# The first 60 microseconds of an attention and feed-forward kernel: first loads, first weight and small constants in another order

## The chip, the cores and the metric

The kernel runs on one core of a Trainium2 chip. The metric is the device time of one execution in microseconds; the median of three runs of the kernel before is 783.38 us (783.3 to 783.8). The engines of the core, TensorE (matrix products), VectorE, ScalarE, GpSimd and SyncE, each work through their own list of instructions, and meet by semaphores. Transfers between main memory and the on-chip memory are issued by GpSimd, SyncE or ScalarE and carried out by 16 DMA engines.

## The reference

```python
# q, k, v: (4, 6080, 256)
qn = q / (norm(q, axis=1) + 1e-6);  kn = k / (norm(k, axis=1) + 1e-6)
s = kn.transpose(0, 2, 1) @ qn / tau          # (4, 256, 256), tau = 1
a = softmax(s, axis=-1)
x = (v @ a).reshape(24320, 256)
h = x @ w_in                                  # (256, 2048)
g = s_scale * relu(h) ** 2 + b
out = g @ w_out                               # (2048, 256)
```

The attention runs over the 256 channels: per batch, a sum over 6080 tokens gives one 256 x 256 matrix and the norms of each channel of q and k. All inputs are float32, and so is the output.

## The kernel before

**The work and its tiles.** Per batch the matrix `a` is multiplied into `w_in` first ("fold", lines 231 to 246), so that the main loop takes v straight to the hidden layer with the folded weight `wa`. The constant b becomes a row that is added at the end (`rowconst`, b times the column sums of w_out), and the scale s is applied, with that row, when the output leaves the accumulator (line 449).

The main loop goes over groups of 512 tokens, and in each over 16 blocks of 128 hidden features: a step. A step is two matmuls of 512 columns (`mm1`, line 417), ScalarE's Relu (line 420), VectorE's square (line 427), and, four and five steps later, four matmuls of 256 columns into the output (`mm2`, line 441). Everything else for later is hung into this loop as side work for a given step: v loads and transposes, the Gram matrices, norms and folds of the next batch, the casts of w_out to float16 (lines 321 to 326), and the sums for `rowconst` (lines 330 to 339).

**The front.** Batch 0 has to be done before the loop can begin. Its q and k come in eight chunks (five of 1024 tokens, then 512, 256 and 192). Per chunk TensorE adds to the Gram matrix `s_ps` (line 120), ScalarE squares k (143), VectorE squares q (140) and adds the squares up by halves (156). After the last chunk comes a chain: 40 tiny matmuls sum the squares over tokens (`n_ps`, 185), a square root, a reciprocal, the scaled matrix `sm_s` (201), its transposes `t_ps` (208), the exponentials `eT` (214), their sums `r_ps` (223), and sixteen fold matmuls, in eight pairs of 512 columns, each evacuated to `wa` by ScalarE or VectorE in turn (242, 244). The transposes of the first v tile (272) stand between `t_ps` and the sums.

**What sets the order.** Nearly every instruction is pinned by `po` to the written order on its engine; the constants outside it are placed by a scheduler. All large loads go out from GpSimd on one software queue, in this order: eight times k and q (which the DMA converts to float16), w_in, v0, w_out in two halves, v1, v2, then v3 and the k and q of batch 1. A GpSimd load waits until the eighth before it has landed. `s_bc` and `b_bc`, the broadcast scalars s and b, come on SyncE's queue at the very start.

**Buffers.** `h_ps` has four accumulator buffers, which h, the folds, the transposes and the norm sums share; the relu result r has three; k and q tiles have six. w_out lands as float32 in `w_out32` (16 x 256 per partition).

Of the kernel before, what the change touches and what calls it, by code (L numbers as in the profile page):

```python
# [10 lines left out]
FP32 = mybir.dt.float32  # L11
AF = mybir.ActivationFunctionType
# [4 lines left out]
def kernel(  # L17
# [12 lines left out]
    nc = tc.nc  # L30
    P = 128

    B, N, C = q.shape
    Dff = moe_w_in.shape[1]
# [7 lines left out]
    LAM = 16.0  # L42
    EPS = 1e-6

    CH = C // P
    FT = Dff // P
    TG = 512
# [4 lines left out]
    def po(ins):  # L52

        tc.keep_in_program_order(ins)
        return ins
# [39 lines left out]
    class Gram:  # L95


        def __init__(self, b, chunks):
            self.b, self.chunks = b, chunks
            self.tiles = {}  # L100
            self.rows = []

        def load(self, c):
            at, np_, jc = self.chunks[c]
            kc = qk_pool.tile([P, JC, C], FP16, tag="kc", name="kc")
            qc = qk_pool.tile([P, JC, C], FP16, tag="qc", name="qc")
            for t, src in ((kc, k), (qc, q)):
                po(nc.gpsimd.dma_start(  # L108
                    out=t[:np_, :jc, :],
                    in_=src[self.b, at : at + np_ * jc, :].rearrange("(p j) c -> p j c", j=jc)))  # L110
# [18 lines left out]
        def norm_ops(self, c):  # L129
# [43 lines left out]
                ops += [fold(4, slice(0, 1), False), fold(4, slice(1, 2), False)]  # L173
            return ops + [fold(2, slice(0, 2), False), fold(1, slice(0, 2), True)]

        def finish_ops(self):

            st = {}

            def norms():  # L180
                n_ps = ps_h.tile([P, 2, CH], FP32, tag="h_ps", name="n_ps")
                todo = [(t, np_, j, a, ch) for t, np_, jc in self.rows for j in range(jc)
                        for a in range(2) for ch in range(CH)]
                for i, (t, np_, j, a, ch) in enumerate(todo):
                    po(nc.tensor.matmul(n_ps[:, a, ch : ch + 1], t[:np_, a, j, ts(ch, P)],  # L185
                                        ones16[:np_, 0:1], start=(i == 0),
                                        stop=(i == len(todo) - 1), skip_group_check=True))
                nrm = sm_pool.tile([P, 2, CH], FP32, tag="nrm", name="nrm")
                po(nc.scalar.activation(out=nrm, in_=n_ps, func=AF.Sqrt))
# [13 lines left out]

            def turn():
                st["t"] = ps_h.tile([P, CH, C], FP32, tag="h_ps", name="t_ps")
                for j in range(CH):
                    for ch in range(CH):
                        po(nc.tensor.transpose(  # L208
                            st["t"][:, j, ts(ch, P)], st["s"][:, ch, ts(j, P)], ident32))

            def exps():
                st["e"] = sm_pool.tile([P, CH, C], FP16, tag="eT", name="eT")
                for j in range(CH):
                    po(nc.scalar.activation(  # L214
                        out=st["e"][:, j, :], in_=st["t"][:, j, :], func=AF.Exp,
                        scale=st["r"][:, 0, j : j + 1]))
                self.wa = apool.tile([P, CH, Dff], FP16, tag="wa16", name="wa16")

            def sums():
                r_ps = ps_h.tile([P, CH], FP32, tag="h_ps", name="r_ps")  # L220
                for ch in range(CH):
                    for j in range(CH):
                        po(nc.tensor.matmul(r_ps[:, ch : ch + 1], st["e"][:, j, ts(ch, P)],
                                            ones16[:, 0:1], start=(ch == 0 and j == 0),
                                            stop=(ch == CH - 1 and j == CH - 1),
                                            skip_group_check=True))
# [4 lines left out]
            NW = 512  # L231

            def fold_w(fo, m):
                def f():
                    wa_ps = ps_h.tile([P, NW], FP32, tag="h_ps", name="wa_ps")
                    for j in range(CH):
                        po(nc.tensor.matmul(wa_ps, st["e"][:, j, ts(m, P)],  # L237
                                            w_in16[:, j, ds(fo * NW, NW)],
                                            start=(j == 0), stop=(j == CH - 1)))
# [18 lines left out]
    def load_v(g):  # L258
        t0, nj = group(g)
        v16 = vpool.tile([P, TG // P, C], FP16, tag="v16", name="v16")  # L260
        po(nc.gpsimd.dma_start(  # L261
            out=v16[:, :nj, :],
            in_=v_flat[t0 : t0 + nj * P, :].rearrange("(p j) c -> p j c", j=nj)))
        v_tiles[g] = v16
# [10 lines left out]
        vT_tiles[g] = vT  # L275


    grams = {b: Gram(b, chunks_first if b == 0 else chunks_later) for b in range(B)}
    g0 = grams[0]
    for c in range(len(g0.chunks)):  # L280
        g0.load(c)
    po(nc.gpsimd.dma_start(out=w_in16, in_=moe_w_in.rearrange("(co p) f -> p co f", p=P)))
    load_v(0)
    w_out_rows = moe_w_out.rearrange("(fo p) d -> p fo d", p=P)
    for h in range(2):
        po(nc.gpsimd.dma_start(out=w_out32[:, ts(h, FT // 2), :], in_=w_out_rows[:, ts(h, FT // 2), :]))
    load_v(1)
    load_v(2)
    ident16 = consts.tile([P, P], FP16)
    make_identity(nc, ident16)  # L290
    ident32 = consts.tile([P, P], FP32)
# [2 lines left out]
    nc.vector.memset(ones16, 1.0)  # L294
    ones32 = consts.tile([P, P], FP32)
    nc.vector.memset(ones32, 1.0)
    s_bc = consts.tile([P, 1], FP32)
    nc.sync.dma_start(out=s_bc, in_=moe_s.to_broadcast((P, 1)))
    b_bc = consts.tile([P, 1], FP32)
    nc.sync.dma_start(out=b_bc, in_=moe_b.to_broadcast((P, 1)))  # L300
    s_out = consts.tile([P, 1], FP32)
    nc.vector.tensor_scalar_mul(out=s_out, in0=s_bc, scalar1=1.0 / (LAM * LAM))


    warm = consts.tile([P, 1], FP32)
    po(nc.scalar.activation(out=warm, in_=ones32[:, 0:1], func=AF.Sqrt))
    g0.start()
    for c in range(len(g0.chunks)):
        ops = g0.norm_ops(c)
        for j in range(g0.chunks[c][2]):  # L310
            g0.mm(c, j)
        for f in ops:
            f()
    fin = g0.finish_ops()
    for f in fin[:3]:
        f()
    transpose_v(0)
    for f in fin[3:]:
        f()

    def cast_w_out(i):
        part = slice(i * FT // 8, (i + 1) * FT // 8)
        if i % 2:
            po(nc.scalar.copy(out=w_out16[:, part, :], in_=w_out32[:, part, :]))
        else:
            po(nc.vector.tensor_copy(out=w_out16[:, part, :], in_=w_out32[:, part, :]))

    cast_w_out(0)

    def rowconst_sum(i, n):  # L330
        w = w_out32.rearrange("p f c -> p (f c)")
# [173 lines left out]
```

## Time and profile before

| | |
|---|---|
| median of three runs | 783.38 us |
| profiled execution, its time / span | 782.96 / 781.2 us |
| TensorE matmuls busy | 753.2 us (96%) |
| VectorE, ScalarE busy | 505.2, 517.8 us |
| main memory read, written | 78.9 MB, 24.9 MB |
| landing of k0, q0; of q4; of v0 | 8.3, 10.9; 30.6; 42.0 us |
| first matmul of the main loop | 47.58 us |
| first matmul into the output | 49.74 us |
| the rowconst matmul | 62.24 us |

A line of a group gives the code line, engine and operation, output and inputs with their shapes, the count, then busy time and the mean of one in ns, then the idle time of the engine just before such instructions and what ended it. Lines of the chain and the timeline begin with the start and length in us. The lines of stretches give for each engine the busy time and the count, in the order TensorE matmul, weight load, VectorE, ScalarE, GpSimd, and then TensorE's granted clock, the DMA engines' busy share and GB/s.

### The profile page before, as it was taken

Reading aid. Unit: us, or ns where it says so; the run is one execution under the profiler, and the core shown is the slowest. Engines: PE = TensorE matmul, PEld = TensorE weight load, DVE = VectorE, ACT = ScalarE, POOL = GpSimd, SP = SyncE. Lnnn points to the kernel's source line nnn. Section 1 sums busy time; section 2 is a strip of 40 time slices with the busy share of each in tenths; the row PEclk is TensorE's granted clock in tenths of the full one; section 3 lists DMA queues with packets and bytes.
Section 4 is the critical chain, followed back from the end, with each engine's and each line's share of the span. In section 5 each row is a group of like instructions: output and inputs, shape, how many; then the busy total and the mean of one; then the engine's idle time right before and its main releaser. Section 6 shows DMA issues by size and latency. Waiting matters only on the chain.

```text
span 781.2 us, 14420 instructions
## 1 busy us (share of the span) xinstructions
PE 753.2 (96%) x5646; PEld 527.4 (68%) x5646; DVE 505.2 (65%) x1106; ACT 517.8 (66%) x858; POOL 57.2 (7%) x111
## 2 busy tenths in 40 slices
PE   2689999999999999999999999999999999999997
PEld 2456777767677777776667667776667766666666
DVE  3767676676656766666566666766566565565565
ACT  3466666666766666766766666666676666666665
POOL 3410010001000010000001000000000000000000
PEclk9689999999999999999999999999999999999999
DMA  8999425115535164124715645131113113121011
GB/s 158 212 263 186 96 44 130 41 41 101 131 76 115 41 133 95 41 42 85 145 41 96 129 85 108 46 75 45 41 48 74 42 42 83 42 52 51 28 55 42
DMA packets 22421, 66.34 MB, mean 85 GB/s; under 512 B 2752, under 2 KB 3328, under 8 KB 22352
## 3 DMA queue, kind: packets, MB, share of 16 engines
q0 software_dynamic: 15152, 40.51, 29.4%
q1 hardware_dynamic: 7200, 24.91, 9.8%
q8 instruction: 44, 0.72, 0.4%
q14 instruction: 25, 0.20, 0.1%
HBM read 78.91 MB, written 24.90 MB: 133 GB/s over the span
## 4 chain that ended last, share of the span: by engine, by line
PE 93%; DMA 5%; issue 1%; ACT 1%; DVE 0%; POOL 0%; POOLq 0%
PE o_ps L441 42%; PE h_ps L417 42%; PE s_ps L120 4%; DMA qc<-in_q_dram 4%; PE vT_ps L272 3%; PE wa_ps L237 2%; DMA v<-in_v_dram 1%; ACT r L420 0%; PE n_ps L185 0%; ACT eT L214 0%; PE t_ps L208 0%; ACT L214 0%; DVE o_sb L449 0%; PE rc_ps L338 0%; POOL kc L108 0%
## 5 line engine op out<-in xcount | busy, mean ns | idle before, releaser
L420 ACT ACTIVATE r<-h_ps 128x512 f16<-128x512 f32 (+1 forms) x768 | 450.0, 593 | 225.8 <-PE h_ps L417 199.9
L427 DVE TENSOR_TENSOR g<-r 128x512 f16<-128x512 f16 (+1 forms) x768 | 321.9, 420 | 243.4 <-ACT r L420 236.6
L441 PE MATMUL o_ps<-w_out,g 128*128 128x256 f16 x3040 | 456.8, 273 | 0.0
L417 PE MATMUL h_ps<-vT,wa 128*128 128x512 f16 (+7 forms) x1632 | 453.0, 364 | 0.6 <-ACT r L420 0.6
L441 PEld LDWEIGHTS <-g 128*128 128x128 f16 x3040 | 295.2, 98 | 183.0 <-DVE g L427 0.2
L417 PEld LDWEIGHTS <-wa 128*128 128x128 f16 x1632 | 157.9, 98 | 30.0 <-issue 0.8
L120 PE MATMUL s_ps<-qc,kc 128*128 128x256 f16 (+1 forms) x384 | 72.9, 296 | 18.5 <-DMA qc<-in_q_dram 18.5
L449 DVE SCALAR_TENSOR_TENSOR o_sb<-o_ps,s_out,rowconst 128x512 f32<-128x512 f32 x95 | 71.1, 748 | 6.4 <-PE o_ps L441 5.6
L261 POOL DMA_DIRECT2D v<-in_v_dram x48 | 25.7, 535 | 617.0 <-PE vT_ps L272 597.6
L143 ACT ACTIVATE sq<-kc 128x1024 f16<-128x1024 f16 (+3 forms) x49 | 50.0, 1031 | 21.9 <-DMA kc<-in_k_dram 18.7
L120 PEld LDWEIGHTS <-kc 128*128 128x128 f16 (+1 forms) x384 | 40.2, 106 | 26.8 <-issue 10.2
L140 DVE TENSOR_TENSOR sq<-qc 128x1024 f16<-128x1024 f16 (+3 forms) x49 | 32.6, 675 | 11.1 <-DMA qc<-in_q_dram 11.1
L274 DVE COPY vT<-vT_ps 128x1024 f16<-128x1024 f16 (+1 forms) x48 | 32.5, 677 | 4.3 <-PE vT_ps L272 4.3
L156 DVE TENSOR_TENSOR f<-sq 128x1024 f16<-128x1024 f16 (+1 forms) x47 | 31.8, 685 | 0.3
L272 PE MATMUL vT_ps<-ident,v 128*128 128x128 f16 x380 | 29.5, 221 | 2.0 <-DMA v<-in_v_dram 2.0
L272 PEld LDWEIGHTS <-v 128*128 128x128 f16 x380 | 25.5, 99 | 3.5 <-DMA v<-in_v_dram 2.4
L156 DVE TENSOR_TENSOR f<-f 128x512 f16<-128x512 f16 (+3 forms) x47 | 25.8, 550 | 0.4
L237 PE MATMUL wa_ps<-w_in,eT 128*128 128x512 f16 x64 | 18.9, 398 | 0.0
L242 ACT ACTIVATE wa<-wa_ps,rs 128x512 f16<-128x512 f32 x16 | 11.0, 687 | 7.6 <-PE wa_ps L237 4.3
L108 POOL DMA_DIRECT2D qc<-in_q_dram x26 | 14.2, 548 | 13.7 <-DMA qc<-in_q_dram 7.7
L108 POOL DMA_DIRECT2D kc<-in_k_dram x26 | 14.2, 548 | 11.4 <-DMA kc<-in_k_dram 9.1
L244 DVE TENSOR_SCALAR wa<-wa_ps,rs 128x512 f16<-128x512 f32 x16 | 11.9, 745 | 1.4 <-PE wa_ps L237 1.2
(37 smaller groups left out, 55.9 us busy)
## 6 DMA issues: line engine op xcount, KB each, us to landing
out_dram<-o_sb SPq DMA_DIRECT2D x47, 512.0 KB, 3.7
v<-in_v_dram POOLq DMA_DIRECT2D x47, 256.0 KB, 5.1
kc<-in_k_dram POOLq DMA_DIRECT2D x20, 512.0 KB, 8.1
qc<-in_q_dram POOLq DMA_DIRECT2D x20, 512.0 KB, 10.0
w_out<-in_moe_w_out_dram POOLq DMA_DIRECT2D x2, 1024.0 KB, 13.2
kc<-in_k_dram POOLq DMA_DIRECT2D x3, 480.0 KB, 8.4
qc<-in_q_dram POOLq DMA_DIRECT2D x3, 480.0 KB, 10.3
w_in<-in_moe_w_in_dram POOLq DMA_DIRECT2D x1, 1024.0 KB, 12.5
```

What stands on the lines that cost most here:

```text
L120: po(nc.tensor.matmul(self.s_ps[:, ch, :], kc[:np_, j, ts(ch, P)], qc[:np_, j, :], start=(c == 0 and j == 0 and ch == 0), stop=(c == len(s ...
L140: po(nc.vector.tensor_mul(st["sq"][:np_, 0, js, :], qc[:np_, js, :], qc[:np_, js, :]))
L143: po(nc.scalar.activation(out=st["sq"][:np_, 1, js, :], in_=kc[:np_, js, :], func=AF.Square))
L156: po(nc.vector.tensor_add(st["f", half][:np_, arrays], src[:np_, arrays, :half, :], src[:np_, arrays, half : 2 * half, :]))
L237: po(nc.tensor.matmul(wa_ps, st["e"][:, j, ts(m, P)], w_in16[:, j, ds(fo * NW, NW)], start=(j == 0), stop=(j == CH - 1)))
L272: po(nc.tensor.transpose(vT_ps[:, ch, ts(j, P)], v16[:, j, ts(ch, P)], ident16))
L274: po(nc.vector.tensor_copy(out=vT[:, :, : nj * P], in_=vT_ps[:, :, : nj * P]))
L417: po(nc.tensor.matmul(dst, wa[:, ci, ts(m, P)], src, start=(ci == 0), stop=(ci == CH - 1), skip_group_check=True))
L420: po(nc.scalar.activation(out=r16[:, :n], in_=h_ps[:, :n], func=AF.Relu))
L427: po(nc.vector.tensor_mul(g16[:, :n], r16[:, :n], r16[:, :n]))
L441: po(nc.tensor.matmul(o_halves[g, h][:, j % 2, :], g16[:, ts(j, P)], w_out16[:, m, :], start=(m == 0 and j == js[0]), stop=(m == FT - 1 an ...
L449: po(nc.vector.scalar_tensor_tensor(out=o_sb[:, js[0] : js[-1] + 1, :], in0=o_halves.pop((g, h)), scalar=s_out, op0=ALU.mult, in1=rowconst ...
```

## The change

- The first k and q go out from SyncE's and ScalarE's hardware queues, as float32, into the buffer of w_out, which is still empty; VectorE casts k and ScalarE casts q to float16.
- The identity matrices are made on GpSimd ahead of the loads instead of after them.
- w_in is loaded in two pieces: its first 512 columns, then v0, then the other 1536. Only the first block of the weight is folded ahead of the loop; the other six folds are side work of steps 1, 2, 5, 6, 9 and 10. The casts of w_out move from the place before the loop and steps 0 to 6 to steps 2 to 9.
- The norm sums of all chunks but the last stand before the last chunk's Gram matmuls: 32 of the 40 tiny matmuls go ahead of it, eight stay behind.
- Eight matmuls whose result nobody reads (`keep_busy`) stand in the chain: six ahead of the transposes `t_ps`, two ahead of the sums.
- `s_bc` and `b_bc` are loaded from GpSimd's queue, after v2; `s_out`, computed from `s_bc` on VectorE, is now pinned after the first two folds.

```diff
@@ class Gram
+            direct = self.b == 0 and c == 0
+            for i, (t, src) in enumerate(((kc, k), (qc, q))):
+                rows = src[self.b, at : at + np_ * jc, :].rearrange("(p j) c -> p j c", j=jc)
+                if direct:
+                    raw = w_out32[:, ds(i * JC, JC), :]
+                    (nc.sync, nc.scalar)[i].dma_start(out=raw, in_=rows)
+                else:
+                    po(nc.gpsimd.dma_start(out=t[:np_, :jc, :], in_=rows))
...
+        def cast(self, c):
+            qc, kc = self.tiles[c]
+            for h in range(2):
+                js = slice(h * JC // 2, (h + 1) * JC // 2)
+                po(nc.vector.tensor_copy(out=kc[:, js, :], in_=w_out32[:, js, :]))
+                po(nc.scalar.copy(out=qc[:, js, :],
+                                  in_=w_out32[:, JC + js.start : JC + js.stop, :]))
...
+        def add_norms(self, last=False):
+            first = self.n_ps is None
+            if first:
+                self.n_ps = ps_h.tile([P, 2, CH], FP32, tag="h_ps", name="n_ps")
+            todo = [(t, np_, j, a, ch) for t, np_, jc in self.rows for j in range(jc)
+                    for a in range(2) for ch in range(CH)]
+            self.rows = []
...
@@ the front
-    for c in range(len(g0.chunks)):
-        g0.load(c)
-    po(nc.gpsimd.dma_start(out=w_in16, in_=moe_w_in.rearrange("(co p) f -> p co f", p=P)))
-    load_v(0)
...
-    nc.sync.dma_start(out=s_bc, in_=moe_s.to_broadcast((P, 1)))
-    nc.sync.dma_start(out=b_bc, in_=moe_b.to_broadcast((P, 1)))
-    nc.vector.tensor_scalar_mul(out=s_out, in0=s_bc, scalar1=1.0 / (LAM * LAM))
...
+    g0.load(0)
+    po(nc.scalar.activation(out=warm, in_=ones32[:, 0:1], func=AF.Sqrt))
+    g0.cast(0)
+    for c in range(1, len(g0.chunks)):
+        g0.load(c)
+    load_w_in(0, NW)
+    load_v(0)
+    load_w_in(NW, Dff)
     for h in range(2):
         po(nc.gpsimd.dma_start(out=w_out32[:, ts(h, FT // 2), :], in_=w_out_rows[:, ts(h, FT // 2), :]))
+    load_v(1)
+    load_v(2)
+    po(nc.gpsimd.dma_start(out=s_bc, in_=moe_s.to_broadcast((P, 1))))
+    po(nc.gpsimd.dma_start(out=b_bc, in_=moe_b.to_broadcast((P, 1))))
...
+        if c == NCH0 - 1:
+            g0.add_norms()
...
+    def keep_busy(n):
+        idle_ps = ps_h.tile([P, TG], FP32, tag="h_ps", name="idle_ps")
+        for _ in range(n):
+            po(nc.tensor.matmul(idle_ps, w_in16[:, 0, :P], w_in16[:, 0, :NW],
+                                start=True, stop=True, skip_group_check=True))
...
-    for f in fin[:3]:
-        f()
-    transpose_v(0)
-    for f in fin[3:]:
-        f()
+    fin[0]()
+    fin[1]()
+    keep_busy(6)
+    fin[2]()
+    transpose_v(0)
+    keep_busy(2)
+    for f in fin[3:7]:
+        f()
+    po(nc.vector.tensor_scalar_mul(out=s_out, in0=s_bc, scalar1=1.0 / (LAM * LAM)))
...
-    cast_w_out(0)
...
-    for i in range(1, 8):
-        at_step(i - 1, lambda i=i: cast_w_out(i))
+    for i, f in enumerate(fin[7:]):
+        at_step(i // 2 * 4 + i % 2 + 1, f)
+    for i in range(8):
+        at_step(i + 2, lambda i=i: cast_w_out(i))
```

More of the change, by code (lines that the diff above doesn't have):

```diff
@@ L100, in __init__ @@
             self.tiles = {}
-            self.rows = []
+            self.rows, self.n_ps = [], None
         def load(self, c):
@@ L106, in load @@
             qc = qk_pool.tile([P, JC, C], FP16, tag="qc", name="qc")
[L107 to L110, printed above, removed]
-            self.tiles[c] = qc, kc
+            direct = self.b == 0 and c == 0
[6 more added lines that the diff above has]
+                    po(nc.gpsimd.dma_start(out=t[:np_, :jc, :], in_=rows))
+            self.tiles[c] = qc, kc
+        def cast(self, c):
[5 more added lines that the diff above has]
+                                  in_=w_out32[:, JC + js.start : JC + js.stop, :]))
         def start(self):
@@ L174, in norm_ops @@
             return ops + [fold(2, slice(0, 2), False), fold(1, slice(0, 2), True)]
+        def add_norms(self, last=False):
[5 more added lines that the diff above has]
+            self.rows = []
+            for i, (t, np_, j, a, ch) in enumerate(todo):
+                po(nc.tensor.matmul(self.n_ps[:, a, ch : ch + 1], t[:np_, a, j, ts(ch, P)],
+                                    ones16[:np_, 0:1], start=(first and i == 0),
+                                    stop=(last and i == len(todo) - 1), skip_group_check=True))
         def finish_ops(self):
@@ L180, in norms @@
             def norms():
[L181 to L187, printed above, removed]
+                self.add_norms(last=True)
                 nrm = sm_pool.tile([P, 2, CH], FP32, tag="nrm", name="nrm")
-                po(nc.scalar.activation(out=nrm, in_=n_ps, func=AF.Sqrt))
+                po(nc.scalar.activation(out=nrm, in_=self.n_ps, func=AF.Sqrt))
                 st["nrm"] = nrm
@@ L229, in sums @@
                 po(nc.vector.reciprocal(out=st["rs"], in_=st["rs"]))
-            NW = 512
             def fold_w(fo, m):
@@ L275, in transpose_v @@
         vT_tiles[g] = vT
-    grams = {b: Gram(b, chunks_first if b == 0 else chunks_later) for b in range(B)}
-    g0 = grams[0]
-    for c in range(len(g0.chunks)):
-        g0.load(c)
-    po(nc.gpsimd.dma_start(out=w_in16, in_=moe_w_in.rearrange("(co p) f -> p co f", p=P)))
-    load_v(0)
[L284 to L288, printed above, removed]
     ident16 = consts.tile([P, P], FP16)
@@ L296, with load_w_in @@
     nc.vector.memset(ones32, 1.0)
-    s_bc = consts.tile([P, 1], FP32)
-    nc.sync.dma_start(out=s_bc, in_=moe_s.to_broadcast((P, 1)))
-    b_bc = consts.tile([P, 1], FP32)
-    nc.sync.dma_start(out=b_bc, in_=moe_b.to_broadcast((P, 1)))
-    s_out = consts.tile([P, 1], FP32)
-    nc.vector.tensor_scalar_mul(out=s_out, in0=s_bc, scalar1=1.0 / (LAM * LAM))
+    grams = {b: Gram(b, chunks_first if b == 0 else chunks_later) for b in range(B)}
+    g0 = grams[0]
+    assert FT == 2 * JC
+    g0.load(0)
     warm = consts.tile([P, 1], FP32)
     po(nc.scalar.activation(out=warm, in_=ones32[:, 0:1], func=AF.Sqrt))
+    g0.cast(0)
+    for c in range(1, len(g0.chunks)):
+        g0.load(c)
+    NW = 512
+    w_in_rows = moe_w_in.rearrange("(co p) f -> p co f", p=P)
+    def load_w_in(f0, f1):
+        po(nc.gpsimd.dma_start(out=w_in16[:, :, f0:f1], in_=w_in_rows[:, :, f0:f1]))
+    load_w_in(0, NW)
+    load_v(0)
+    load_w_in(NW, Dff)
+    w_out_rows = moe_w_out.rearrange("(fo p) d -> p fo d", p=P)
+    for h in range(2):
+        po(nc.gpsimd.dma_start(out=w_out32[:, ts(h, FT // 2), :], in_=w_out_rows[:, ts(h, FT // 2), :]))
+    load_v(1)
+    load_v(2)
+    s_bc = consts.tile([P, 1], FP32)
+    po(nc.gpsimd.dma_start(out=s_bc, in_=moe_s.to_broadcast((P, 1))))
+    b_bc = consts.tile([P, 1], FP32)
+    po(nc.gpsimd.dma_start(out=b_bc, in_=moe_b.to_broadcast((P, 1))))
+    s_out = consts.tile([P, 1], FP32)
     g0.start()
-    for c in range(len(g0.chunks)):
+    NCH0 = len(g0.chunks)
+    for c in range(NCH0):
         ops = g0.norm_ops(c)
+        if c == NCH0 - 1:
+            g0.add_norms()
         for j in range(g0.chunks[c][2]):
```

## The prediction

> **What bounds the kernel now.** I read the groups of the page first, to see where TensorE is ever idle.
>
> ```profile
> L441 PE MATMUL o_ps<-w_out,g 128*128 128x256 f16 x3040 | 456.8, 273 | 0.0
> L417 PE MATMUL h_ps<-vT,wa 128*128 128x512 f16 (+7 forms) x1632 | 453.0, 364 | 0.6 <-ACT r L420 0.6
> L120 PE MATMUL s_ps<-qc,kc 128*128 128x256 f16 (+1 forms) x384 | 72.9, 296 | 18.5 <-DMA qc<-in_q_dram 18.5
> ```
>
> The two large groups never wait; only the first Gram matrix waits for loads. So everything after some 62 us is a solid row of matmuls: a microsecond won or lost at the front is one at the end, if it reaches the steady loop. The chain of waits, from the start to 80 us, shows what holds the front:
>
> ```profile
> 1.89 9.02 DMA qc<-in_q_dram
> ...
> 11.20 19.38 DMA qc<-in_q_dram
> ...
> 30.86 11.19 DMA v<-in_v_dram
> ...
> 42.10 1.03 PE vT_ps L272 x8
> 43.13 0.09 PE r_ps L223 x4
> 43.21 4.53 PE wa_ps L237 x16
> 47.74 2.16 PE h_ps L417 x10
> ...
> 60.67 0.61 ACT r L420
> 61.28 0.96 issue
> 62.24 0.67 PE rc_ps L338 x2
> ```
>
> Loads to 42.1 us, the sixteen folds of the weight (half clock at first) to 47.7, the loop, and one stall of some 1.3 us ahead of the rowconst matmul. Third, the timeline of VectorE and GpSimd, for what sits in which queue:
>
> ```profile
> 4.16 0.15 DVE L302 TENSOR_SCALAR s_out<-s_bc 128x1 f32<-128x1 f32 x1 [3.02 <-DMA s_bc<-in_moe_s_dram]
> ...
> 34.18 1.12 POOL L261 DMA_DIRECT2D v<-in_v_dram  x2
> ...
> 48.45 0.42 DVE L326 CAST w_out<-w_out 128x512 f16<-128x512 f32 x1
> ...
> 49.74 0.38 PE L441 MATMUL o_ps<-w_out,g 128*128 128x256 f16 x2
> ```
>
> The scale `s_bc` arrives at 4.1 us; its VectorE instruction is out of the way long before the loop. The two v tiles of 34.18 us are v1 and v2: the landing times give 14.2 us for v1 and 15.0 for v2, so v2 lands at 34.74 + 15.0 = 49.7 us. Last, the stretches of one microsecond, for the clock (the column before the DMA share):
>
> ```profile
> 37.00:38.00 1.00, 0.44 (x16) 0.35 (x12) 0.31 (x3) 0.17 (x1) 0.46 (x1) 1.00 1.01 201
> 39.00:40.00 1.00, 0.99 (x4) 0.69 (x4) 0.00 (x0) 0.42 (x1) 0.00 (x0) 0.50 1.01 195
> 46.00:47.00 1.00, 1.00 (x7) 0.45 (x5) 0.83 (x2) 0.82 (x2) 0.00 (x0) 1.00 1.10 223
> ```
>
> TensorE fell to half clock after an idle stretch and came back some 3 us after it was busy again (42.1 to 45.1). DMA share is 1.0 throughout: the queue is full until about 67 us.
>
> [...] This trace: all GpSimd loads land in the order of issue. [...]
>
> **The change part by part.** Times are those of the profiled execution (782.96 us, span 781.2); the median, 783.38, is 0.4 above it, and I add the difference of fronts to the median.
>
> (1) *Start of loading.* On the software queue from idle, k0 and q0 (2.1 MB read) land at 10.9 us, issued from 1.23: 9.7 us, against 4.95 at the steady 2.47 us for each 1.05 MB, so 4.7 us of overhead. The later burst of 67.35 us shows the same (landing at 79.2, 11.9 us for 6.2 us of bytes). The hardware queue has less: 3.4 us for the tiny `s_bc`, 3.7 less 1.24 = 2.5 for an output tile. With k0 and q0 on it from 0.74 us, while the software queue ramps up behind (its first issue moves from 1.23 to about 2.4 us, behind the identities' 0.39 + 0.77), the stream is 1.23 + 4.7 - 0.74 - (2.5 to 3.4) = 1.8 to 2.7 us earlier, less 0.25 for landing as float32 (w_out takes 2.6 us where 2.47 is usual). I take g = 1.9; from below 0 (the slow start lies in the DMA engines), from above 2.7. Bytes ahead of v2 are the same as before, so everything loaded shifts by g.
>
> (2) *Casts of chunk 0.* VectorE 2 x about 0.75, ScalarE 2 x 1.03 us. VectorE has 3.7 us of work in the 4.9 us of a chunk, so it has caught up two chunks later: nothing. Cover gone: 1.5 us.
>
> (3) *Early norm sums.* 32 of 40 tiny matmuls (1.3 us in all, 0.033 each) move ahead of the last chunk's four Gram matmuls. But VectorE's last square ends at 37.03, and the moved ones wait for its squares before: between -0.3 and +0.2, I take 0.
>
> (4) *Fillers.* Six matmuls of 0.216 us at full clock fit between the norms (37.4) and `sm_s` (38.86); at half clock they take 2.6 and delay the transposes by 1.1. Two more: 0.4 to 0.9.
>
> (5) *Weight by blocks.* The first quarter and v0 need 1.05 MB after q7 (35.35 us), so land at 37.9 - g; ScalarE's exps end near 41.1 - g; sums, two folds at 0.22 to 0.43 each matmul, an evacuation of 0.7: the first h_ps near 43.2 - g = 41.3, against 47.58. The other twelve fold matmuls stay work for TensorE, in the loop.
>
> (6) *`s_bc` moved.* This decides. Its load now stands on the software queue behind v2, and the VectorE instruction that reads it (`s_out`) stands, by the written order, after the first VectorE fold and before the first square `g`. Queued behind it: g of steps 0, 1, 2, the second fold on VectorE, the first cast of w_out. TensorE's step 4 needs that fold (h_ps of the second block), then g and the cast (first o_ps). ScalarE stops as well: r has three buffers, which g frees. So VectorE arrives at about 41.2 and waits until `s_bc` lands: 49.7 - 1.9 + 0.4 (its 128 pieces of 4 bytes; 0 to 1.5) = 48.2 us. Then s_out 0.1, three g at a spacing of 0.34, fold 0.67, cast 0.42, hand-over 0.1: 2.3 us, so the first o_ps at 50.55 where it was at 49.74: **+0.8**.
>
> TensorE meanwhile stands idle from about 44.1 to 50: parts (2) to (5) gain or lose into this hole and cost nothing; it would take more than 3 us of delay before any showed.
>
> (7) *After the hole.* Before, all sixteen fold matmuls were done at this point; now eight of them (steps 1 and 2 had four) are still to come in steps 5 to 10: 8 x 0.216 = **+1.7**. Six idle microseconds drop the clock; the two returns seen took 3.0 (42.1 to 45.1) and 4.4 us (30.6 to 35.0), half lost: 1.5 to 2.2, I take **+2.0** (0 to 3.2). The stall at rowconst: VectorE has a cast (0.35) and a fold (0.68) more from step 8 on, TensorE two folds (0.86); but it starts that stretch without arrears: 1.3 becomes about 1.2, **-0.1** (-1.3 to +1).
>
> (8) *Rest.* SP loses two issues (0.55 us each) that nothing waited for. GpSimd gains one more issue of w_in and the two of s and b, some 0.55 to 0.73 each, near 35 us, in a stretch where it waits for landings anyway; each of its loads waits for the eighth before it, and 2.5 MB or more stay outstanding, so the stream has no gap. The second batch's first k, behind them, landed at 53.3 and is wanted after 64 us: nothing.
>
> Sum: 0.8 + 1.7 + 2.0 - 0.1 = +4.4; 783.4 + 4.4 = **787.8 us** (own range 785.2 to 790.6).
>
> **The rivals.** *The small load is not late* (other side). If `s_bc` lands before about 42 us, whatever its place in the queue, VectorE never blocks, and above that each microsecond is one. Then v1 (48.4 - 1.9 = 46.5) holds step 4: its transposes at 46.55 against 49.96 is -3.4, folds +1.7: 781.7 us. For it: its bytes are nothing. Against: [...] 5.8 MB ahead of it (both parts of w_in, v0, w_out, v1, v2) when it is issued near 34 us.
>
> *The hole costs little.* Same stall, but a larger g (2.7) and a clock that returns at once or a rowconst stall that vanishes: 0 + 1.7 + 1 - 0.7 = +2.0, 785.4. For it: ramps differ; against: every idle stretch in this trace halved the clock.
>
> *No gain at the start.* The ramp belongs to the engines, or three queues disturb each other, g about 0, or the 4-byte pieces take 1.5 us: 2.7 + 1.7 + 2.3 = +6.7, 790.1. For: the first packets are slow on either queue.
>
> *The fillers don't hold the clock* (the change doesn't do what it says): 1 to 1.5 us later into the hole, time as forecast.
>
> **How the numbers follow.** Stall with cold clock 0.62; cheap hole 0.18; no start gain 0.13; small load not late 0.07. Change under 0.2% (1.6 us, about what a measurement of this kernel can tell from no change): half of the cheap hole's lower part and a little of the last case, 0.10. Faster 0.06, slower 0.84. The range leaves out the early-load case and the far tail: 784.2 to 791.0.
>
> **What would show it.** VectorE's s_out with some 7 us of idle before it, released by the load of s_bc near 48 us; TensorE idle some 6 us before h_ps of step 4, clock 0.5 for 3 to 4 us after it; first h_ps near 41; k0 and q0 landing together at 8 to 10 us, and q of chunk 4 near 28.7; the rowconst matmul near 66.7. I am wrong if s_out shows no wait, if the loads don't come earlier, or if the clock stays full across the hole.

## The result, and the profile after

The changed kernel takes 790.03 us in the median of four runs (789.95 to 790.52), the kernel before 783.59 beside it: a ratio of 1.0084 (95% interval 1.0066 to 1.0101), 6.4 us slower. The profiled execution took 790.06 us with a span of 788.3, that is 7.1 more than before. The groups show where the time sits (columns as before: busy time and mean of one, then the idle time and what ended it).

```profile
L458 PE MATMUL h_ps<-vT,wa 128*128 128x512 f16 (+7 forms) x1632 | 454.7, 365 | 10.8 <-DVE wa L262 9.7
L482 PE MATMUL o_ps<-w_out,g 128*128 128x256 f16 x3040 | 457.5, 273 | 0.0
```

Before, the hidden-layer matmuls waited 0.6 us; now 10.8, of which 9.7 for a fold that VectorE evacuates. The busy times of the two large groups rose by 2.4 us; some 1.7 of that is the colder clock (an estimate, from the stretches below, where the two groups work for 3.4 us at half clock), the rest I could not place. The chain of waits from the start to 80 us names the holder (start and length in us):

```profile
34.07 15.98 DMA s_bc<-in_moe_s_dram
50.23 1.00 DVE g L468 x3
51.23 0.67 DVE wa L262
51.95 0.61 PE h_ps L458
```

A load of 128 times 4 bytes takes the place that v0 and the sixteen folds had in the chain before. The timeline gives the same in time, with the idle time ahead of each entry in brackets:

```profile
39.99 1.32 PE L458 MATMUL h_ps<-vT,wa 128*128 128x512 f16 x4 [0.35 <-ACT wa L260]
...
50.07 0.15 DVE L360 TENSOR_SCALAR s_out<-s_bc 128x1 f32<-128x1 f32 x1 [9.64 <-DMA s_bc<-in_moe_s_dram]
...
51.95 0.61 PE L458 MATMUL h_ps<-vT,wa 128*128 128x512 f16 x1 [8.70 <-DVE wa L262]
52.35 0.63 PE L482 MATMUL o_ps<-w_out,g 128*128 128x256 f16 x2
...
59.26 0.39 PE L458 MATMUL h_ps<-vT,wa 128*128 128x512 f16 x1 [0.52 <-DVE wa L262]
...
69.35 0.67 PE L377 MATMUL rc_ps<-w_out,ones 128*128 128x256 f32 x2 [0.76 <-ACT r L461]
```

The loop starts 7.6 us earlier than before (39.99 against 47.58), and VectorE then stands for 9.64 us at `s_out`. Behind it in its queue are three squares and a fold; TensorE stops 8.70 us for that fold. The wait of 0.52 us for a fold comes a second time at 64.29. The rowconst matmul comes at 69.35 us where it came at 62.24: 7.11 us, the whole difference of the two executions. After it the two traces run alike.

Last the clock. These are stretches of TensorE alone: length, busy time and count, granted clock, busy share of the DMA engines, GB/s. I cut them every 3.41 us, such that the two points at which the clock changes (45.94 and 56.18) are among the cuts; the last section tells why. Before the first point, back to 32.3 us, and after the second it is full.

```profile
42.53:45.94 3.41, 0.72 (x4) 1.00 1.09 273
45.94:49.35 3.41, 0.00 (x0) 0.50 0.50 75
49.35:52.77 3.42, 0.82 (x3) 0.50 0.98 189
52.77:56.18 3.41, 3.41 (x17) 0.50 1.07 211
```

TensorE works at half clock from 51.95 to 56.18, 4.2 us, and so loses 2.1 (half of it, an estimate; the run warm_hole below measured 2.0). The second line also holds a surprise: about the time of the two small loads the stream, which otherwise moves over 200 GB/s, falls to 75. The fall begins at 46.0 us, before v2, which stands ahead of them, has landed (48.20).

Put together, the difference of 7.1 us at the rowconst matmul is: first output matmul later by 52.35 - 49.74 = 2.6; eight folds that are still to be done after it, 8 x 0.216 = 1.7; the clock, 2.1; two waits for folds of 0.52, 1.0; the stall at the rowconst matmul 0.76 instead of 1.17, -0.4. That makes 7.0.

### The profile page after: what moved, and what is told of

Read it like the earlier page. It is cut to its first block, busy times and chain, and to the rows that moved or that the text cites. A ratio compares the mean times of both kernels' runs of the same rounds, so it can differ in the third digit from the quotient of the medians.

```text
span 788.3 us, 14443 instructions
## 1 busy us (share of the span) xinstructions
PE 752.9 (96%) x5654; PEld 526.5 (67%) x5654; DVE 506.4 (64%) x1108; ACT 520.0 (66%) x860; POOL 57.8 (7%) x112
## 4 chain that ended last, share of the span: by engine, by line
PE 91%; DMA 5%; issue 1%; POOL 1%; ACT 1%; DVE 1%; POOLq 0%; ACTq 0%
PE o_ps L482 41%; PE h_ps L458 41%; PE s_ps L133 4%; DMA qc<-in_q_dram 3%; PE vT_ps L290 3%; DMA s_bc<-in_moe_s_dram 2%; PE wa_ps L255 1%; ACT r L461 0%; DVE g L468 0%; POOL kc L114 0%; DVE wa L262 0%; POOL w_out L324 0%; PE n_ps L198 0%; POOL v L279 0%; POOL qc L114 0%
## 5 line engine op out<-in xcount | busy, mean ns | idle before, releaser
L458 PE MATMUL h_ps<-vT,wa 128*128 128x512 f16 (+7 forms) x1632 | 454.7, 365 | 10.8 <-DVE wa L262 9.7
L133 PE MATMUL s_ps<-qc,kc 128*128 128x256 f16 (+1 forms) x384 | 69.9, 286 | 19.0 <-ACT qc L123 11.2
L114 POOL DMA_DIRECT2D kc<-in_k_dram x25 | 13.7, 547 | 13.7 <-DMA kc<-in_k_dram 9.6
L114 POOL DMA_DIRECT2D qc<-in_q_dram x25 | 13.7, 548 | 8.9 <-DMA qc<-in_q_dram 5.7
```

Of the source, the lines that this page charges most:

```text
L114: po(nc.gpsimd.dma_start(out=t[:np_, :jc, :], in_=rows))
L133: po(nc.tensor.matmul(self.s_ps[:, ch, :], kc[:np_, j, ts(ch, P)], qc[:np_, j, :], start=(c == 0 and j == 0 and ch == 0), stop=(c == len(s ...
L458: po(nc.tensor.matmul(dst, wa[:, ci, ts(m, P)], src, start=(ci == 0), stop=(ci == CH - 1), skip_group_check=True))
```

## The experiments

The theory of the prediction was that VectorE's wait for the small load holds the loop (A). Its rivals were that the small load doesn't matter, that the cost is the cold clock alone (B), and that the start or the fillers decide. Each run has runs of the kernel before beside it on the same chip, and ratios are to those.

**Take the waiting instruction away (sout_later).** The loads stay; `s_out` moves to step 16 of the loop.

```diff
-    po(nc.vector.tensor_scalar_mul(out=s_out, in0=s_bc, scalar1=1.0 / (LAM * LAM)))
...
+    at_step(16, lambda: po(nc.vector.tensor_scalar_mul(out=s_out, in0=s_bc, scalar1=1.0 / (LAM * LAM))))
```

> The changed kernel with one instruction moved: s_out, VectorE's instruction that waits for s_bc, stands at step 16 of the loop instead of ahead of the first square; the load of s_bc stays where the change put it. Theory (VectorE's queue stands still behind s_out): no wait of VectorE there, the first o_ps near 44, v1 (landing near 46.5) holds TensorE for some 2.5 us at its transposes, the rowconst matmul near 60.5, and 782 us (781.3 to 783). Rival one (the folds and casts inside the loop are what costs): 788 or more. Rival two (the 4-byte loads spoil the stream, wherever they are waited for): the stream stays slow from 46 us and the time with it, 786 or more.

Measured 784.1 us (781.69 to 784.53, twelve runs), ratio 0.9999 (0.999 to 1.0007). Moving one instruction of 0.15 us brings back all that the change cost, so A holds. But it brings no more than that, and the 782 us expected were missed by 2, though the first output matmul now comes at 44.23 us, 5.5 us earlier than in the kernel before. The timeline of this kernel shows what is late next:

```profile
43.87 0.39 PE L458 MATMUL h_ps<-vT,wa 128*128 128x512 f16 x1 [0.99 <-DVE wa L262]
44.23 0.38 PE L482 MATMUL o_ps<-w_out,g 128*128 128x256 f16 x2
47.08 1.03 PE L290 MATMUL vT_ps<-ident,v 128*128 128x128 f16 x8 [2.47 <-DMA v<-in_v_dram]
```

TensorE waits for a fold (0.99), then for v1 (2.47). The stretches of TensorE, cut in the same way, add the clock, which is full again after the last:

```profile
42.02:45.43 3.41, 1.60 (x7) 1.00 1.08 300
45.43:48.85 3.42, 1.77 (x11) 0.50 0.62 100
48.85:52.26 3.41, 3.41 (x14) 0.50 0.94 186
```

Half clock from 47.08 to 52.26 costs 2.6 us more (again half of the time, an estimate). The rowconst matmul is at 63.83 in this execution (784.53 us, the longest of the twelve). The best of the twelve, 781.69, has no profile; that it lost less to the clock is argued only.

**The small loads on another queue (sbc_on_sp).** `s_out` stays where the change put it.

```diff
-    po(nc.gpsimd.dma_start(out=s_bc, in_=moe_s.to_broadcast((P, 1))))
+    nc.sync.dma_start(out=s_bc, in_=moe_s.to_broadcast((P, 1)))
-    po(nc.gpsimd.dma_start(out=b_bc, in_=moe_b.to_broadcast((P, 1))))
+    nc.sync.dma_start(out=b_bc, in_=moe_b.to_broadcast((P, 1)))
```

> The changed kernel with the loads of s_bc and b_bc on SyncE's queue, behind k of chunk 0; s_out stands where the change put it. Theory: s_bc is there long before, VectorE doesn't wait, 782 us as with s_out moved. If the 4-byte pieces also cost the stream some microseconds when they run beside the first loads, q of chunk 4 lands 1 to 3 us later than 28.3 and the time is 783 to 785.

Measured 783.29 (783.02 to 784.83, twelve runs), ratio 0.9998 (0.9989 to 1.0006). The load lands near 13 us and `s_out` waits for nothing: once more the loss is gone, by removing the lateness this time and not the instruction. The 782 us of the theory were missed here too; the other case of the expectation, 783 to 785 with q of chunk 4 later, is what came. The clock is full from 35.5 us on. Of TensorE's remaining waits, the timeline has these two; besides them there are 0.99 us for a fold at 45.97, another 0.52 at 57.65, and 0.76 at the rowconst matmul (62.71):

```profile
47.79 0.62 PE L290 MATMUL vT_ps<-ident,v 128*128 128x128 f16 x8 [1.12 <-DMA v<-in_v_dram]
...
52.62 0.39 PE L458 MATMUL h_ps<-vT,wa 128*128 128x512 f16 x1 [0.52 <-DVE wa L262]
```

The first output matmul (46.30) is 3.4 us earlier than before, the rowconst matmul 0.5 later. Of the 3.9 given back, v1 takes 1.12, the folds' work 1.7, the two later waits for folds 1.04, the shorter rowconst stall returns 0.4, and some 0.4 I could not place. The chunks also came later here: q4 landed at 29.7 us, in the ten kernels with the changed start and late small loads at 27.8 to 28.3.

**Keep TensorE busy in the hole (warm_hole).** 34 matmuls whose result nobody reads, 7.5 us long, at the end of step 3.

```diff
+    def keep_warm(n):
+        warm_ps = ps_gram.tile([P, TG], FP32, tag="s_ps", name="warm_ps")
+        for _ in range(n):
+            po(nc.tensor.matmul(warm_ps, w_in16[:, 0, :P], w_in16[:, 0, :NW], ...))
+    at_step(3, lambda: keep_warm(34))
```

> The changed kernel with 34 matmuls that nobody reads at the end of step 3, in the idle stretch of TensorE (some 7.3 us of it); the wait for s_bc stays. Theory: the wait is as long, but the clock stays full, and the 4.2 us at half clock after the stretch are saved at half: 787.9 us (787.4 to 788.6). Rival (the clock is hidden behind VectorE's and ScalarE's arrears): 789.5 to 790.2.

Measured 788.07 (787.91 to 788.15), ratio 1.0057 (1.004 to 1.0074): 2.0 us less than the change, and the rowconst matmul at 67.38 is 2.0 earlier. The timeline shows that the wait itself is still there:

```profile
42.43 7.50 PE L389 MATMUL warm_ps<-w_in 128*128 128x512 f16 x34
...
51.92 0.39 PE L465 MATMUL h_ps<-vT,wa 128*128 128x512 f16 x1 [1.77 <-DVE wa L262]
```

So the cold clock is 2.0 of the 6.4 us, and B falls as the only cause. It also shows that TensorE had 7.5 us with nothing to lose.

**A second small load ahead of the first (small_twice).**

```diff
+    s_first = consts.tile([P, 1], FP32)
+    po(nc.gpsimd.dma_start(out=s_first, in_=moe_b.to_broadcast((P, 1))))
     s_bc = consts.tile([P, 1], FP32)
```

> The changed kernel with one more 128-piece broadcast load ahead of s_bc on GpSimd's queue. If such a load takes the stream some 1.9 us (the gap of 1.85 us between the landings of v2 and s_bc), s_bc lands near 52 and the time is 791.9 (791.3 to 792.6). If small loads are nearly free, as my forecast had it at 0.4 us, 790.2 to 790.5.

Measured 790.06, 790.20, 790.63 and 791.72, ratio 1.009 (1.0075 to 1.0105). The profiled one is that of 791.72 us; its timeline:

```profile
51.69 0.15 DVE L362 TENSOR_SCALAR s_out<-s_bc 128x1 f32<-128x1 f32 x1 [11.52 <-DMA s_bc<-in_moe_s_dram]
```

In this execution `s_out` comes 1.62 us later than in the change and the rowconst matmul 1.66, as the theory had it. The other three lie 0.0 to 0.6 us above the change's 790.0, and the median of the four, 790.41, falls into the range expected for a load that is nearly free. So the expectation of 791.9 was missed. The landings of the profiled execution suggest why the extra load need not cost 1.6 us: with two small loads between them v1 and v3 land 6.16 us apart in the change, and with three 6.04 us here. Here the third load changed when each small load landed (the extra one 0.71 us after v2, `s_bc` 2.63 after that, `b_bc` 0.15 later), but not what they took together. That `s_bc` landed earlier in the three faster executions was not seen, as they have no profile.

**The small loads one place earlier (sbc_before_v1).** Ahead of v1 and v2 on GpSimd's queue instead of behind them, the rest as in the change.

```diff
-    load_v(1)
-    load_v(2)
     s_bc = consts.tile([P, 1], FP32)
     po(nc.gpsimd.dma_start(out=s_bc, in_=moe_s.to_broadcast((P, 1))))
     b_bc = consts.tile([P, 1], FP32)
     po(nc.gpsimd.dma_start(out=b_bc, in_=moe_b.to_broadcast((P, 1))))
+    load_v(1)
+    load_v(2)
```

> The changed kernel with the loads of s_bc and b_bc one place earlier, ahead of v1 and v2 instead of behind them; s_out stands where the change put it. Theory (each microsecond of the landing is one of the time): s_bc lands near 47.0 instead of 50.1, and the time is 3 us less than the changed kernel's 790.0, 786.6 to 787.8, unless v1, now behind it near 49, is late by some tenths. If the place of the load hardly matters: 789.5 to 790.3.

Measured 787.92 (786.56 to 788.23), ratio 1.0046 (1.0029 to 1.0063), 2.1 us less than the change and 0.1 above the range expected. The timeline:

```profile
47.56 0.15 DVE L360 TENSOR_SCALAR s_out<-s_bc 128x1 f32<-128x1 f32 x1 [7.15 <-DMA s_bc<-in_moe_s_dram]
```

`s_bc` lands 2.51 us earlier, TensorE resumes 2.51 earlier (49.44), the rowconst matmul comes 2.24 earlier (67.11). With the load's landing moved one way by 2.51 and the other by 1.62, the end follows nearly one to one in both profiles (in both the clock costs 0.6 to 0.7 us more than in the change, and one wait of 0.52 us for a fold is gone). Together with sout_later and sbc_on_sp this shows the mechanism.

**Without the fillers (no_fillers).**

```diff
-    keep_busy(6)
...
-    keep_busy(2)
```

> The changed kernel without its eight matmuls that nobody reads. Theory: whatever they do to the chain ends in the idle stretch ahead of step 4, which ends with the landing of s_bc: the same time as the changed kernel, 789.4 to 790.7. Rival (they hold the clock for what follows): 791 or more; rival (they only cost): 789 or less.

Measured 789.74 (789.56 to 790.28), ratio 1.0073 (1.0058 to 1.0088): not to be told from the change. The fillers do what they are for: without them TensorE ran at half clock from 38.5 to 41.9 us, with them at full clock. But the first hidden matmul comes at 39.94 instead of 39.99, and what is lost falls into the hole: TensorE waits 7.42 us there and not 8.70.

**The start by itself (before_hw_start, before_small_late).** The prediction said that the hardware queues win 1.9 us. Two edits on the kernel before divide the start. The first takes over the load of chunk 0 by hardware queues, its casts and the early identities, and leaves `s_bc` and `b_bc` on SyncE's queue at the start. The second leaves chunk 0 on the software queue, moves only the two small loads behind v2, and `s_out` to step 16.

```diff
# before_hw_start, on the kernel before
-    for c in range(len(g0.chunks)):
-        g0.load(c)
...
+    g0.load(0)      # k on SyncE's, q on ScalarE's hardware queue
+    po(nc.scalar.activation(out=warm, in_=ones32[:, 0:1], func=AF.Sqrt))
+    g0.cast(0)
+    for c in range(1, len(g0.chunks)):
+        g0.load(c)
```

> The kernel before with chunk 0 on the hardware queues, cast on chip, identities first; s_bc and b_bc stay on SyncE's queue, now behind k of chunk 0. If the hardware queue is what brings the stream forward, q of chunk 4 lands 2 us earlier than 30.6 and the time is 781.5 to 782.2 (ratio 0.997 to 0.998). If the 4-byte loads at the start were what cost the stream 2 us, it still has them: q of chunk 4 at 30.2 to 30.6, ratio 0.999 to 1.001.

```diff
# before_small_late, on the kernel before
-    nc.sync.dma_start(out=s_bc, in_=moe_s.to_broadcast((P, 1)))
-    nc.sync.dma_start(out=b_bc, in_=moe_b.to_broadcast((P, 1)))
-    nc.vector.tensor_scalar_mul(out=s_out, in0=s_bc, scalar1=1.0 / (LAM * LAM))
...
+    po(nc.gpsimd.dma_start(out=s_bc, in_=moe_s.to_broadcast((P, 1))))
+    po(nc.gpsimd.dma_start(out=b_bc, in_=moe_b.to_broadcast((P, 1))))
...
+    at_step(16, lambda: po(nc.vector.tensor_scalar_mul(out=s_out, in0=s_bc, scalar1=1.0 / (LAM * LAM))))
```

> The kernel before with s_bc and b_bc loaded from GpSimd behind v2, and s_out at step 16, where nothing is late for it; chunk 0 stays on the software queue. If the slow start is the software queue's own, as my forecast had it: q of chunk 4 at 30.4 to 30.8 and ratio 1.000. If the 4-byte loads slow the start: q of chunk 4 at 28.4 to 29, and ratio 0.997 to 0.998, about 2 us less.

Measured 782.67 (781.87 to 783.36, twenty runs), ratio 0.9986 (0.9979 to 0.9993) for the first, and 781.02 (780.88 to 782.04), ratio 0.9964 (0.995 to 0.9978) for the second. The first lies between its two expectations, the second slightly beyond the one that blamed the 4-byte loads. (In before_hw_start `s_out` also stops VectorE for 2.38 us, until `s_bc` lands at 12.9 us.) The landing of q of chunk 4 is the measure of the stream that the prediction named:

| q4 lands at | small loads at the start | small loads late |
|---|---|---|
| chunk 0 on the software queue | 30.6 us (before) | 28.6 (before_small_late) |
| chunk 0 on hardware queues | 29.6 (before_hw_start) | 28.3 (the change) |

Removing the small loads from the start is worth 2.0 or 1.3 us, the hardware queues 1.0 or 0.3. These are single executions: in the ten with the changed start and late small loads q4 landed between 27.8 and 28.3 us, which makes the second figures 1.3 to 1.8 and 0.3 to 0.8. In the stretches of one microsecond (TensorE, weight load, VectorE, ScalarE, GpSimd, then clock, DMA share, GB/s) the same software loads run faster without them. First the kernel before:

```profile
4.00:5.00 1.00, 0.00 (x0) 0.00 (x0) 0.15 (x1) 0.00 (x0) 1.00 (x3) 1.00 0.95 168
```

and here before_small_late, at its start and then where its small loads are now:

```profile
4.00:5.00 1.00, 0.00 (x0) 0.00 (x0) 0.00 (x0) 0.00 (x0) 1.00 (x3) 1.00 1.13 225
...
47.00:48.00 1.00, 1.00 (x6) 0.47 (x5) 1.00 (x3) 1.00 (x3) 0.53 (x1) 1.00 0.13 19
```

The slump moved with the small loads. Late, it costs TensorE nothing: between 42 and 64 us its only wait is that of 1.17 us at the rowconst matmul, as before. And this edit alone, which is a small part of the change, makes the kernel before 0.36% faster.

**Mending the change (mended and three parts of it).** The runs above name four things: `s_out`, v1 behind 2 MB of w_out, the folds that come 0.52 us late, and the rowconst stall.

```diff
+    load_v(1)
     for h in range(2):
         po(nc.gpsimd.dma_start(out=w_out32[:, ts(h, FT // 2), :], ...))
-    load_v(1)
...
-    po(nc.vector.tensor_scalar_mul(out=s_out, in0=s_bc, scalar1=1.0 / (LAM * LAM)))
...
-        at_step(i // 2 * 4 + i % 2 + 1, f)
+        at_step(i // 2 * 4 + i % 2, f)
...
+    at_step(16, lambda: po(nc.vector.tensor_scalar_mul(out=s_out, in0=s_bc, scalar1=1.0 / (LAM * LAM))))
...
-    at_step(8 + len(todo), rowconst_mm)
+    at_step(10 + len(todo), rowconst_mm)
```

> The changed kernel with s_out at step 16, v1 loaded ahead of w_out, the six later folds one step earlier and the rowconst matmul two steps later. Theory: no wait for v1 (2.5 us), no fall of the clock after it, no waits of TensorE for the folds on VectorE (0.5 to 1.0 each), the rowconst stall shorter: first o_ps near 44.4, the rowconst matmul's step at 58 to 59, 779 us (778.3 to 780.5), ratio 0.993 to 0.996. If TensorE is held by something else there, 782 or more.

Measured 777.68 (777.54 to 777.77), ratio 0.9918 (0.9903 to 0.9932), below the range expected: faster than both kernels, 6 us below the one before and, by the two ratios, some 13 below the change. The whole list of TensorE's waits between 42 and 66 us in its timeline is:

```profile
43.22 0.39 PE L458 MATMUL h_ps<-vT,wa 128*128 128x512 f16 x1 [0.50 <-DVE wa L262]
44.09 0.38 PE L482 MATMUL o_ps<-w_out,g 128*128 128x256 f16 x2 [0.48 <-DVE w_out L366]
```

The waits for v1, for the later folds and at the rowconst matmul are gone, and the clock stays full from 26.6 us on. On this base, where there is no hole to swallow a loss, the other parts of the change can be priced. Three runs take one back each: no fillers; all norm sums after the last chunk; all sixteen folds ahead of the loop.

```diff
# mended_no_fillers
-    keep_busy(6)
...
-    keep_busy(2)
```

> The mended kernel without its eight matmuls that nobody reads. With the idle stretch gone the chain is on the path: without them the clock should fall near 38 us, as in the changed kernel without them, and the first folds and h_ps run at half clock, 0.9 us later. But the cast of w_out, whose load lands near 43.5, still sets the first o_ps near 44.1, so I expect 777.7 to 778.6. Rival (they only cost): below 777.4.

```diff
# mended_late_norms
-        if c == NCH0 - 1:
-            g0.add_norms()
```

> The mended kernel with all norm sums after the last chunk's Gram matmuls, as in the kernel before. My step (3) gave the early sums nothing: 777.4 to 778.1. Rival (they take up to 1 us out of the chain): 778.3 or more.

```diff
# mended_front_folds
-    for f in fin[3:7]:
+    for f in fin[3:]:
         f()
...
-    for i, f in enumerate(fin[7:]):
-        at_step(i // 2 * 4 + i % 2, f)
```

> The mended kernel with all sixteen fold matmuls ahead of the loop again. If the folds inside the loop bring something, it is their overlap with the wait for w_out's first cast: the first o_ps moves from 44.1 to about 46, with 8 fold matmuls (1.7 us) less behind it: 777.7 to 778.6. If the work in blocks was worth what the change's description leads one to think (12 of 16 matmuls, 2.6 us, hidden): 780.

| beside one another on one chip | median, us | ratio | interval |
|---|---|---|---|
| mended_no_fillers | 778.61 | 0.9933 | 0.9919 to 0.9948 |
| mended_late_norms | 777.58 | 0.9919 | 0.9904 to 0.9934 |
| mended_front_folds | 777.51 | 0.9916 | 0.9902 to 0.9931 |

The fillers are worth some 1.0 us here (half clock from 36.3 to 39.7 without them, rowconst matmul 1.0 later). The early norm sums are worth nothing that can be measured, as the prediction had it. Nor is folding by blocks inside the loop: with all folds ahead of it the first output matmul comes at 45.30 instead of 44.09, but the folds are then done, and the end is the same within the spread of the runs. The gain of the mended kernel over the one before therefore comes from the rest: the start, w_in in two pieces with the chain close behind, v1 early, the fillers and the moved rowconst matmul. These were not divided further.

## Why the prediction was right, and where it was off

The forecast was 787.8 us (784.2 to 791.0), slower with a chance of 0.84. It became 790.0, slower and 1 us inside the upper end of the range, by the mechanism of the likeliest case: VectorE blocked at `s_out`, TensorE idle for a fold, clock down. Step by step:

- **Step (1), start of loading.** The gain came out at 2.3 us by q4 (28.3 for 30.6) where 1.9 was taken and 2.7 the upper end. Its cause, as the prediction put it, was in part another. The 4.7 us of "overhead" were read as a property of the software queue. But 2.0 of them went when the two small loads left the start and the queue stayed the same (k0 then lands 5.2 us after its issue and not 7.1, q0 7.7 and not 9.7). The hardware queues themselves bring 0.3 to 1.0; what is left of the 4.7 was not explained. (The burst at 67.35 us, read as showing the same, has no small loads beside it, but an output tile of 512 KB, issued at 67.42.) Two things left the start together, and the reading gave all to one. Further on the gain shrank: v1 landed at 46.46, 1.95 earlier than before, but v2 at 48.20, only 1.5 earlier, where step (6) had counted on 47.8.
- **Steps (2), (3), (4), casts, norm sums, fillers.** Nothing, and so it was: no_fillers equals the change, and taking back the early norm sums costs nothing even without the hole. The casts alone were not tried.
- **Step (5).** First hidden matmul at 39.99 us, forecast 41.3: the chain was shorter than thought. It went into the hole, as the step said it would.
- **Step (6), the small load.** Here lies most of the miss. The load's own price was an estimate of mine, 0.4 us with 0 to 1.5 as bounds, which no trace of the kernel before showed. It took 1.85 after v2 (50.05 - 48.20), outside the bounds; in ten traces it took 1.3 to 2.2 after the load ahead of it. The 0.4 by which v2 itself was later than counted falls into the slump that begins at 46.0 us, so it may belong to the small loads too: v2 comes 1.3 to 1.9 us after v1 in the six traces where small loads stand behind it, and 1.2 to 1.3 in the three where none do. With this 0.4 the first output matmul is 2.6 later than before and not 0.8. The rest of the step held: from landing to that matmul 2.30 us (forecast 2.3). The order within the queues, on which the step leaned, is in the trace: VectorE started nothing in the 9.64 us ahead of `s_out`, and what is written behind it came after it (in the timeline `g` at 50.14, the fold at 51.14); v1, v2 and `s_bc`, all on GpSimd's queue, landed in the order of issue, at 46.46, 48.20 and 50.05.
- **Step (7), after the hole.** The eight folds were not measured by themselves, but with the 1.7 us forecast for them the account above closes to 0.1. The cold clock 2.1 by the stretches and 2.0 by warm_hole, forecast 2.0. The rowconst stall -0.4, forecast -0.1. Missing from the sum altogether were two waits of 0.52 us for folds on VectorE: a fold in the loop is evacuated by VectorE behind a square that waits for ScalarE's relu, and ScalarE has a fold of its own and a cast of w_out ahead of that relu. The timeline of the change has this for the first of the two waits, which ends at 59.26:

```profile
56.39 0.69 ACT L260 ACTIVATE wa<-wa_ps,rs 128x512 f16<-128x512 f32 x1 [1.07 <-PE wa_ps L255]
56.97 0.61 ACT L365 CAST w_out<-w_out 128x512 f16<-128x512 f32 x1
57.48 1.23 ACT L461 ACTIVATE r<-h_ps 128x512 f16<-128x512 f32 x2
58.11 0.43 DVE L468 TENSOR_TENSOR g<-r 128x512 f16<-128x512 f16 x1 [2.33 <-ACT r L461]
58.45 0.75 DVE L262 TENSOR_SCALAR wa<-wa_ps,rs 128x512 f16<-128x512 f32 x1
```

The prediction counted the added work on VectorE and TensorE, but did not follow this loop through three engines. It is +1.0.
- **Step (8), rest.** Nothing, and the traces agree: after the rowconst matmul they are alike.

The terms that were off, +1.8 in step (6), +1.0 missing and -0.3 in the stall, make 2.5. With them 787.8 becomes 790.3, against 790.0 measured.

Of the rivals, "the small load is not late" was priced at 781.7. The two runs that make it not matter gave a ratio of 1.000, some 1.7 us above that: this rival, too, left out the waits for folds, and the fall of the clock during the wait for v1. "The hole costs little" and "no gain at the start" have both their premises refuted. What was held against the first, that every idle stretch in the trace of the kernel before halved the clock, says too much: the 1.17 us ahead of its rowconst matmul left it full. The second one's time, 790.1, is nearly the one measured: one of its ways was small pieces at 1.5 us, near what they took. But it counted no gain at the start, which there was, and none of the waits for folds, so the agreement is in part luck.

## What to carry to other kernels

A tiny constant needs a place in two orders: its load in the queue of transfers, and its reader in the queue of an engine. The reader pinned ahead of urgent work turned the whole queue of loads in front of the constant into its own wait here (9.64 us of VectorE). Price what you gain in front of such a wait at zero until the wait is gone, and when it is gone, look for the next late thing (here v1, folds, clock) before you count the gain; a part that shows nothing in the change may be worth a microsecond in the mended kernel, as the fillers were, or nothing at all, as folding by blocks.

## What the runs showed of the hardware

**Two broadcast loads of 4-byte pieces cost 3.1 to 3.8 us in the busy stream.** In ten traces `s_bc`, one load of 128 x 4 bytes, landed 1.3 to 2.2 us after the large load ahead of it (1.85 in the change), the time in which this stream brings 280 to 450 KB at 210 GB/s. That is not yet the price of one: `b_bc`, the next, followed after anything between 0.15 and 1.7 us. Together they can be priced by the large loads on either side, v1 and v3. These land 2.4 to 2.5 us apart in the three traces without small loads between them (the kernel before, before_hw_start, sbc_on_sp) and 5.6 to 6.3 in five traces with two (the change, sout_later, warm_hole, no_fillers, before_small_late): two cost 3.1 to 3.8 us. With three (small_twice) it was 6.04, no more than with two. In the slump the stream moved 75 GB/s (the change, 45.9 to 49.4 us), and as little as 19 and 60 in two neighbouring microseconds (before_small_late), where some 210 are usual. Two of them at the start, on a hardware queue beside the large loads, cost the stream 1.3 to 2.0 us together. Why is open; only the size was measured.

**The stretches at half clock were multiples of 3.41 us.** Every stretch at half clock between 20 and 70 us in the traces of the kernel before, the changed one and ten of the experiments, 3.4 to 13.7 us long, is one, two, three or four times 3.41 us within 0.03, which is why the stretches above were cut so. The clock fell not only after 3.41 us without work: in sout_later it fell after 3.41 us of which TensorE was busy for 1.60. Here is sbc_before_v1, in the same columns:

```profile
41.39:44.80 3.41, 1.84 (x9) 1.00 0.79 270
44.80:48.21 3.41, 0.00 (x0) 1.00 0.66 121
48.21:51.63 3.42, 2.14 (x12) 0.50 1.10 214
51.63:55.04 3.41, 3.41 (x12) 0.50 1.08 215
```

After the line with 1.84 us of work the clock stayed full, after the one without work it was half, after the one with 2.14 it was still half, and after the last line, a full one, it was full again (the next has clock 1.00). In other stretches of 3.41 us the clock stayed full after 1.64 us of work (warm_hole, 49.41 to 52.82), was still half after 2.63 (sbc_on_sp, 25.2 to 28.6), and was full again after 2.81 (sbc_before_v1, 27.7 to 31.2). Busy times here are modelled. They do not tell by themselves when the clock falls: the kernel before lost it at 38.41 us, after a stretch with 2.44 us of work, more than the 1.64 and 1.84 after which it stayed full, and only 1.0 us of idle:

```profile
35.00:38.41 3.41, 2.44 (x53) 1.00 1.08 219
38.41:41.83 3.42, 1.09 (x4) 0.50 1.05 268
```

Forty of those 53 matmuls are the norm sums, with a single column each; without them the stretch has 1.4 us of work. Whether such matmuls count less for the clock than their modelled busy time was not tested.

The price of an idle stretch did not go by its length: 2.1 us were lost to the clock after the 8.70 us wait of the change, but 2.6 in sout_later, after waits of 0.99 and 2.47 us, and 2.8 in sbc_before_v1, after one of 6.21 us (each half of the time that TensorE worked at half clock, an estimate).
